# Turning attention probabilities by DMA transposes of 16-bit planes instead of TensorE transposes, in a fused attention and feed-forward kernel

## The chip, the cores and the metric

The kernel runs on one core of one Trainium2 chip. The metric is the device time of one execution in microseconds. Three runs of the kernel before gave 1068.8, 1068.5 and 1068.64 us, a median of 1068.64.

## The reference

Eight batches of eight heads, head size 64. Each head has 512 local and 32 global positions. A local query sees the 32 global keys and the local keys at most 32 positions away; a global query sees all 544 keys. The output of all heads, 512 wide, goes through a feed-forward layer of width 2048 with a squared relu.

```python
    s_g = scale * np.matmul(q_g, k_all.transpose(0, 1, 3, 2))
    out_g = np.matmul(sm(s_g), v_all)
    s_ll = scale * np.matmul(q_l, k_l.transpose(0, 1, 3, 2))
    s_ll = np.where(mask, s_ll, -1000000000.0)
    s_lg = scale * np.matmul(q_l, k_g.transpose(0, 1, 3, 2))
    s_l = np.concatenate([s_lg, s_ll], axis=-1)
    a_l = sm(s_l)
    out_l = np.matmul(a_l, np.concatenate([v_g, v_l], axis=2))
...
    h = np.maximum(x @ w_in, 0.0)
    return (h * h @ w_out).astype(np.float32)
```

All inputs are float32. The kernel multiplies mostly in a rounded 32-bit type (F32R); to keep precision it splits an operand into a rounded part and a remainder (value minus rounded value) and adds the products.

## The kernel before

The 512 local queries of a head are done in two halves, so there are 128 local work items ("heads" t in the code), each with 256 queries in two tiles of 128 and, for each tile, a window of 224 keys. The main loop (L589) runs over slots t = 0 to 145. In slot t the attention of head t goes on beside step m = t - 9 of the feed-forward layer: 17 blocks of 256 positions (16 local ones and one for all global positions) of eight steps each. A step has two first products (`gemm1`, 24 matmuls of 256 columns) and, one slot later, two second products (`gemm2`, 12 of 512 columns).

The first 16 heads are "plain": they multiply in full float32 without a split. From slot 17 on the order on TensorE (PE), VectorE (DVE) and ScalarE (ACT) is that of the program text (`FREE`); GpSimd (POOL) and the SyncE queue (SP), which issues nearly all DMAs, are ordered by the scheduler.

One head passes through these steps. `load_head` (L90) loads queries, keys and values as `raw`, 864 columns, two slots ahead; `split_head` (L125) makes the rounded copy `hi` and the remainders one slot ahead; `scores` (L139) multiplies; `softmax1` to `softmax3` (L156 to L195) add the mask and take the row maximum (DVE), scale the maximum (DVE), take exponentials with their sum (ACT) and normalize (DVE) in one of two buffers `prob`. In the next slot `transposes` (L197) turns `prob` in four TensorE transposes into the PSUM tile `pt`, `pt_split` (L202) and `pt_rest` (L217) make rounded parts `ph` (four ACT copies) and remainders (three DVE subtractions), `av` (L226) multiplies with the values in nine matmuls, and `x_evac` (L252) brings the result to SBUF as `x_h` and `x_l`, the feed-forward layer's input.

A slot's order on TensorE is: transposes of t - 1, scores of t, `gemm1` first half, `gemm1` second half, `av` of t - 1, global scores of t, `gemm2`. On DVE: `softmax1`, `pt_rest`, `softmax3`, the square, `x_evac`, the next head's split.

Global queries of four heads form a set of 128 rows, 16 sets in all. Over the slots after the set is filled come `g_soft`, `g_exp`, `g_norm`, four transposes (`g_tr`, L347) and a fifth (`g_tr_last`), their split (`g_rest`), and two times `g_av` (13 matmuls). A table of due slots and places in the slot, in the loop, gives each its position. `act1` (L459) takes the relu of the first product on ACT; the square is on ACT in six of 16 slots (`SQ`) and on DVE in the others.

Of the kernel before, what the change touches and what calls it, by code (L numbers as in the profile page):

```python
# [9 lines left out]
I32 = mybir.dt.int32  # L10
AF = mybir.ActivationFunctionType
# [10 lines left out]
PK = QC + KC + VC  # L22
# [8 lines left out]
FREE = (17, 17, 17)  # L31
LOOK = 2
SQ = (2, 3, 4, 5, 14, 15)
# [25 lines left out]
def attention_moe(  # L59
# [10 lines left out]
    pe, ve, ac = InOrder(tc, nc.tensor), InOrder(tc, nc.vector), InOrder(tc, nc.scalar)  # L70
# [19 lines left out]
    def load_head(t):  # L90
        if plain(t):
            w_take(1)
            raw = wp.tile([P, 1024], F32, tag="w", name=f"raw{t}")[:, :PK]
        else:
            raw = p2.tile([P, PK], F32, tag="raw", name=f"raw{t}")
        if t == 0:
            nc.sync.dma_start(raw[:, : QC + KC], pk[t, :, : QC + KC])
        else:
            nc.sync.dma_start(raw, pk[t])
        heads[t] = dict(raw=raw)  # L100
# [18 lines left out]
    prob = [cp.tile([P, 2 * WIN], F32, name=f"prob{i}") for i in range(2)]  # L119
# [5 lines left out]
    def split_head(t):  # L125

        hd = heads[t]
        raw = hd["raw"]
        if plain(t):
            return  # L130
        hi = p2.tile([P, PK], F32R, tag="hi", name=f"hi{t}")
        lo = p2.tile([P, QC + 192], F32R, tag="lo", name=f"lo{t}")
        ac.copy(hi, raw)
        ve.tensor_sub(lo, raw[:, KC : KC + QC + 192], f(hi[:, KC : KC + QC + 192]))
        ve.tensor_sub(hi[64:, :KC], raw[64:, :KC], f(hi[64:, :KC]))
        ve.tensor_sub(hi[32:64, PK - 64 :], raw[32:64, PK - 64 :], f(hi[32:64, PK - 64 :]))
        hd["hi"], hd["lo"] = hi, lo
# [18 lines left out]
    def softmax1(t):  # L156
        hd = heads[t]
        hf = (t // 8) % 2
        pr = prob[t % 2]
        st = p2.tile([P, 8], F32, tag="st", name=f"st{t}")  # L160
        for u in range(2):
            m = 2 * hf + u
            ve.tensor_tensor_reduce(
                out=pr[:, WIN * u : WIN * (u + 1)],
                in0=hd["s"][:, u, :],
                in1=masks[:, WIN * m : WIN * (m + 1)],
                scale=1.0,
                scalar=-3.0e38,
                op0=ALU.add,
                op1=ALU.max,  # L170
                accum_out=st[:, u : u + 1],
            )
        ve.tensor_scalar(out=st[:, 2:4], in0=st[:, 0:2], scalar1=-scale(t), scalar2=None, op0=ALU.mult)
        hd["st"] = st

    def softmax2(t):
        st = heads[t]["st"]
        pr = prob[t % 2]
        for u in range(2):
            w_ = pr[:, WIN * u : WIN * (u + 1)]  # L180
            ac.activation(
                out=w_, in_=w_, func=AF.Exp, scale=scale(t), bias=st[:, 2 + u : 3 + u], accum_out=st[:, 4 + u : 5 + u]
            )

    def softmax3(t):
        st = heads[t]["st"]
        pr = prob[t % 2]
        ve.tensor_scalar(out=st[:, 6:8], in0=st[:, 4:6], scalar1=1e-9, scalar2=None, op0=ALU.add)
        ve.reciprocal(out=st[:, 0:2], in_=st[:, 6:8])
        for u in range(2):  # L190
            w_ = pr[:, WIN * u : WIN * (u + 1)]
            if MUL <= t < NPLAIN:
                ac.activation(out=w_, in_=w_, func=AF.Copy, scale=st[:, u : u + 1])
            else:
                ve.tensor_scalar(out=w_, in0=w_, scalar1=st[:, u : u + 1], scalar2=None, op0=ALU.mult)  # L195

    def transposes(t):  # L197
        pr = prob[t % 2]
# [3 lines left out]
    def pt_split(t):  # L202
        hd = heads[t]
        if plain(t):
            pts = p2.tile([P, 512], F32, tag="gh", name=f"pts{t}")
            ac.copy(pts, pt)
            hd["pts"] = pts
            return
        ph = p1.tile([P, 640], F32R, tag="ph", name=f"ph{t}")
        pl = p1.tile([P, 256], F32R, tag="pl", name=f"pl{t}")  # L210
        ac.copy(ph[:, :256], pt[:, :256])
        ac.copy(ph[:64, 256:384], pt[:64, 320:448])
        for r in (0, 32):
            ac.copy(ph[r : r + 32, 384:640], pt[64:96, 256:512])
        hd["ph"], hd["pl"] = ph, pl

    def pt_rest(t):  # L217
        if plain(t):
            return
        ph, pl = heads[t]["ph"], heads[t]["pl"]  # L220
        ve.tensor_sub(pl, pt[:, :256], f(ph[:, :256]))
        ve.tensor_sub(ph[64:, 256:384], pt[:64, 320:448], f(ph[:64, 256:384]))

        ve.tensor_sub(ph[64:, 384:640], pt[64:, 256:512], f(ph[:64, 384:640]))

    def av(t):  # L226
# [11 lines left out]
        else:  # L238
            xa = ps_a.tile([64, HALF], F32, tag="xa", name=f"xa{t}")
            vh, vl, ph, pl = hd["hi"][:, c:], hd["lo"][:, QC:], hd["ph"], hd["pl"]  # L240
            mm = []
            for u in range(2):
                o, vs, ps = xa[:, 128 * u : 128 * u + 128], slice(64 * u, 64 * u + 64), slice(128 * u, 128 * u + 128)
                mm += [(o, vh[:, vs], ph[:, ps]), (o, vl[:, vs], ph[:, ps]), (o, vh[:, vs], pl[:, ps])]
            o = xa[:, 64:192]
            mm += [(o, vh[:, 128:192], ph[:, 256:384]), (o, vl[:, 128:192], ph[:, 256:384])]
            mm.append((xa, vh[:, 192:256], ph[:, 384:640]))
# [91 lines left out]
    def g_norm(t):  # L339
# [17 lines left out]
    def g_tr_last(t):

        if state["gs"] is None:
            state["gs"] = ps_a.tile([P, 416], F32, tag="gs", name=f"gs_{t}")  # L360
        ge = state["gs"][:, 288:]
        pe.transpose(ge, sg[:, (t // 4) % 2, 512:640], ident)
        state["ge"] = ge

    def g_rest(t):
        (pth, gt), ge = state["gpt"], state["ge"]
        ptl = p1.tile([P, 512], F32R, tag="ptl", name=f"ptl{t}")
        ac.copy(pth[:64, 512:], ge[:64, :])
        ve.tensor_sub(ptl, gt, f(pth[:, :512]))
        ve.tensor_sub(pth[64:, 512:], ge[64:, :], f(pth[:64, 512:]))  # L370
# [132 lines left out]
    def evac(blk, tiles=(0, 1)):  # L503
        for i in tiles:
            pool, tag = ((p1, "ot"), (p2, "gl"))[i]
# [83 lines left out]
    for t in range(NSTEP + LAG + 1):  # L589
        m = t - LAG  # L590
        ve.on, ac.on, pe.on = [t >= x for x in FREE]
        prev, run = 1 <= t <= NT, 0 <= m < NSTEP
        live, early = t < NT, t < NPLAIN
        if t < NPLAIN - 8:
            load_head(t + 8)
        if NPLAIN <= t + 2 < NT:
            load_head(t + 2)
        if run:
            w_need(m)
        if prev:  # L600
            transposes(t - 1)
        for job, *args in jobs.pop((t, 5), ()):
            job(*args)
        if live and not early:
            scores(t)
        if run:
            gemm1(m, 0)
        if prev:
            pt_split(t - 1)
        for job, *args in jobs.pop((t, 4), ()):  # L610
            job(*args)
        if live:
            softmax1(t)
            softmax2(t)
        if prev:
            pt_rest(t - 1)
        for job, *args in jobs.pop((t, 3), ()):
            job(*args)
# [7 lines left out]
        if prev:  # L626
            av(t - 1)
# [4 lines left out]
        if live and not early:  # L632
            softmax3(t)
        if run:
            act1(m)
        if prev:
            x_evac(t - 1)
            if plain(t - 1):
                w_take(-1)
        if early:  # L640
            softmax3(t)
        w_tick(t, 1)
        if t + 1 < NT:
            split_head(t + 1)
# [5 lines left out]
        elif t == NT:  # L650
            state["gs"] = None
        if live and t % 4 == 3 and (t // 8) % 2 == 1:
            d = t if t % 8 == 3 else t + 2
            for at, *job in (
# [116 lines left out]
```

## Time and profile before

| | |
|---|---|
| median of three runs | 1068.64 us |
| span of the profiled execution | 1067.0 us |
| PE busy | 1050.4 us (98%) |
| DVE busy | 856.3 us (80%) |
| ACT busy | 753.1 us (71%) |
| POOL busy | 3.9 us, 14 instructions |
| mean DMA rate | 91 GB/s |

The profiled execution's span runs from its first to its last instruction; the time measured from outside contains it. Busy time is the sum of an engine's instruction spans; neighbouring matmuls overlap in the pipeline, so starts, not durations, tell what a matmul costs. All instructions issued through the in-order helper carry line L52, so groups are told apart by their tiles' names. PEld is TensorE's weight load. In a row of a group, the numbers behind the bar are busy us and mean ns of one, then idle time before them and what ended it.

### The profile page before, as it was taken

The numbers are of one execution on the slowest core, as the hardware profiler recorded it, in microseconds if no ns is written. First come the engines' busy times: TensorE is split into PE (matmuls) and PEld (weight loads), VectorE is DVE, ScalarE is ACT, GpSimd is POOL, SyncE is SP. The second block draws the span as 40 slices with busy tenths as digits, with TensorE's granted clock in tenths as the row PEclk, the third lists the DMA queues.
The fourth block names the chain that finished last, engine by engine and source line by source line (L and its number), as shares of the span: only waits on it lengthen the run. The fifth ranks groups of instructions, "written<-read, shape, count | busy, mean of one in ns | idle before, by whom it ended". The sixth has DMA issues, their size and how long they took to land.

```text
span 1067.0 us, 21142 instructions
## 1 busy us (share of the span) xinstructions
PE 1050.4 (98%) x7568; PEld 941.7 (88%) x7568; DVE 856.3 (80%) x2687; ACT 753.1 (71%) x1901; POOL 3.9 (0%) x14
## 2 busy tenths in 40 slices
PE   7999999999999999999999999999999999999998
PEld 6776889999998989998999989999999989999896
DVE  5698988898888989988888888888888888874321
ACT  5898877778777776778777777777777787774322
POOL 1000000000000000000000000000000000000000
PEclk9999999999999999999999999999999999999999
DMA  9772132223222322222322222223221322201000
GB/s 372 310 263 74 57 106 76 71 80 98 68 89 64 103 65 83 74 91 77 94 71 82 86 72 76 90 66 100 78 89 55 94 86 66 88 29 33 13 20 20
DMA packets 54312, 96.78 MB, mean 91 GB/s; under 512 B 4288, under 2 KB 29376, under 8 KB 54208
## 3 DMA queue, kind: packets, MB, share of 16 engines
q1 hardware_dynamic: 54064, 95.37, 27.2%
q8 instruction: 60, 0.98, 0.4%
q14 instruction: 44, 0.36, 0.1%
q10 hardware_dynamic: 144, 0.07, 0.0%
HBM read 86.51 MB, written 8.91 MB: 89 GB/s over the span
## 4 chain that ended last, share of the span: by engine, by line
PE 87%; ACT 7%; DVE 4%; issue 1%; DMA 0%; ACTq 0%
PE o L52 33%; PE h L52 32%; PE xa L52 7%; PE s L52 6%; PE pt L52 5%; PE gxo L52 2%; PE gs L52 2%; ACT prob L52 1%; DVE prob L52 1%; ACT r L52 1%; ACT ph L52 1%; ACT hi L52 1%; ACT ot L52 1%; PE gt L52 1%; ACT sg L52 0%
## 5 line engine op out<-in xcount | busy, mean ns | idle before, releaser
L52 PE MATMUL h<-x_h,ws 128*128 128x256 f32 x2048 | 388.9, 283 | 0.0
L52 PEld LDWEIGHTS h<-x_h,ws 128*128 128x128 f32 x2048 | 327.0, 191 | 0.5
L52 PE MATMUL o<-ws,gh 128*128 128x512 f32 x1024 | 321.3, 395 | 0.0
L52 PE MATMUL h<-x_l,ws 128*128 128x256 f32 x1024 | 289.1, 282 | 0.1
L52 PEld LDWEIGHTS o<-ws,gh 128*128 128x128 f32 x1024 | 185.5, 188 | 34.6
L52 PE MATMUL o<-ws,gl 128*128 128x512 f32 x512 | 202.6, 396 | 0.0
L52 PEld LDWEIGHTS h<-x_l,ws 128*128 128x128 f32 x1024 | 195.9, 191 | 0.9 <-DVE x_l L52 0.4
L52 ACT CAST ph<-pt 128x256 fp32r<-128x256 f32 x448 | 141.1, 341 | 67.7 <-PE pt L52 60.8
L52 ACT ACTIVATE prob<-prob,st 128x224 f32<-128x224 f32 x270 | 127.8, 475 | 61.2 <-DVE st L52 59.1
L52 ACT ACTIVATE r<-h 128x512 f32<-128x512 f32 x136 | 81.4, 599 | 112.3 <-PE h L52 112.3
L52 PEld LDWEIGHTS o<-ws,gl 128*128 128x128 f32 x512 | 96.2, 188 | 22.7
L52 DVE CUSTOM_DVE_ANT_0 prob<-s,con 128x224 f32<-128x224 f32 x256 | 90.0, 386 | 24.5 <-PE s L52 23.2
L52 DVE TENSOR_TENSOR gl<-r,gh 128x512 fp32r<-128x512 f32 x128 | 87.9, 686 | 23.3 <-ACT gh L52 20.5
L52 ACT CAST hi<-raw 128x864 fp32r<-128x864 f32 x112 | 102.5, 915 | 1.4
L52 DVE TENSOR_TENSOR r<-h,r 128x512 f32<-128x512 f32 x82 | 56.7, 692 | 51.9 <-ACT r L52 50.6
L52 PE MATMUL xa<-ph,hi 128*64 128x128 f32 x448 | 87.3, 238 | 1.6 <-DVE ph L52 1.2
L52 DVE TENSOR_TENSOR hi<-raw,hi 64x352 fp32r<-64x352 f32 x224 | 82.5, 368 | 6.4
L52 ACT CAST gh<-r 128x512 fp32r<-128x512 f32 x128 | 79.1, 618 | 9.1 <-DVE r L52 8.7
L52 DVE TENSOR_TENSOR ph<-pt,ph 64x128 fp32r<-64x128 f32 x224 | 79.6, 355 | 7.0
L52 DVE TENSOR_TENSOR lo<-raw,hi 128x448 fp32r<-128x448 f32 x112 | 69.6, 622 | 15.3 <-ACT hi L52 12.5
L52 PE MATMUL pt<-con,prob 128*128 128x128 f32 (+1 forms) x512 | 78.2, 274 | 0.7 <-ACT prob L52 0.5
L52 DVE TENSOR_SCALAR prob<-prob,st 128x224 f32<-128x224 f32 x242 | 70.7, 334 | 4.1
(80 smaller groups left out, 1572.7 us busy)
## 6 DMA issues: line engine op xcount, KB each, us to landing
raw<-in_pk_dram SPq DMA_DIRECT2D x127, 432.0 KB, 3.2
wr<-in_w_dram SPq DMA_DIRECT2D x32, 512.0 KB, 7.9
gv<-in_vg_dram SPq DMA_DIRECT2D x32, 320.0 KB, 3.3
out_dram<-ot SPq DMA_DIRECT2D x32, 256.0 KB, 2.2
qr<-in_qg_dram SPq DMA_DIRECT2D x31, 64.0 KB, 2.8
out_dram<-ot SPq DMA_DIRECT2D x8, 64.0 KB, 1.7
con<-in_consts_dram SPq DMA_DIRECT2D x2, 224.0 KB, 5.1
raw<-in_pk_dram SPq DMA_DIRECT2D x1, 304.0 KB, 3.2
```

Of the source, the lines that this page charges most:

```text
L52: r = method(*args, **kwargs)
```

## The change

From the 17th head on, and for all global sets, TensorE no longer turns the probabilities. GpSimd copies the two 16-bit halves of each float32 word into two planes (`turn`), one DMA issued from SP transposes the planes, and GpSimd puts the halves together again (`join`). Local probabilities use one buffer each: `prob`, `planes`, `turned`, `joined`. ACT then makes the rounded parts with one copy of 512 columns (`parts`), DVE the remainders with three subtractions (`parts_rest`). `av` moves from the middle of the next slot to its end, behind the second `gemm2`, and `x_evac` into the slot after that. The head's split is cut into queries and keys (`split_qk`, one slot ahead, DVE remainders queued behind `parts_rest`) and values (`split_v`, in the head's own slot); `raw` is 800 columns wide. The row maximum is taken as a minimum of the negated scaled scores, so that its scaling on DVE goes. All squares are on ACT from step 8 on, in the tile `pt`. GpSimd and SP are held to the program's order from slot 17 on too, and a later head's load stands behind the transposing DMA of its slot.

```diff
-FREE = (17, 17, 17)
+FREE = (17, 17, 17, 17, 17)
-SQ = (2, 3, 4, 5, 14, 15)
...
+    def split_qk_rest(t):
+        ve.tensor_sub(hi[64:, :KC], raw[64:, :KC], f(hi[64:, :KC]))
+        ve.tensor_sub(hi[:, QK:], raw[:, KC:QK], f(hi[:, KC:QK]))
+    def split_v(t):
+        raw = heads[t]["raw"]
+        v = heads[t]["v"] = p2.tile([P, 2, 192], F32R, tag="v", name=f"v{t}")
+        ac.copy(v[:, 0, :], raw[:, QK:])
+        ve.tensor_sub(v[:, 1, :], raw[:, QK:], f(v[:, 0, :]))
...
+    def turn(t):
+        words = prob.bitcast(U16).rearrange("p (n h) -> p h n", h=2)
+        to = planes.rearrange("p (h n) -> p h n", h=2)
+        for o, a, n in ((0, 0, WIN), (256, WIN, 96), (384, 320, 128)):
+            po.tensor_copy(to[:, :, o : o + n], words[:, :, a : a + n])
+        sp.dma_start_transpose(out=turned, in_=planes)
+    def join(t):
+        words = joined.bitcast(U16).rearrange("p (n h) -> p h n", h=2)
+        po.tensor_copy(words, turned.rearrange("p (h c) n -> p h (c n)", h=2))
+    def parts(t):
+        ph = heads[t]["ph"] = p1.tile([P, 512], F32R, tag="ph", name=f"ph{t}")
+        ac.copy(ph, joined)
+    def parts_rest(t):
+        ve.tensor_sub(ph[96:, 128:384], joined[64:96, 128:384], f(ph[64:96, 128:384]))
+        ve.tensor_sub(ml[:64, :], joined[:64, 192:320], f(ph[:64, 192:320]))
+        ve.tensor_sub(pl.rearrange("p (c n) -> p c n", c=2), sides(joined), sides(f(ph)))
...
+    def g_turn(t, s):
+        a = p1.tile([P, 1280], U16, tag="pth", name=f"gp{t}")
+        z = p1.tile([P, 10, P], U16, tag="ptl", name=f"gq{t}")
+        words = s.bitcast(U16).rearrange("p (n h) -> p h n", h=2)
+        po.tensor_copy(a.rearrange("p (h n) -> p h n", h=2), words)
+        sp.dma_start_transpose(out=z, in_=a)
+        po.tensor_copy(words, z.rearrange("p (h c) n -> p h (c n)", h=2))
...
-                (d + 2, 1, g_tr),
-                (d + 3, 5, g_tr_last),
-                (d + 3, 4, g_rest),
+                (d + 3, 2, g_parts),
```

TensorE at a slot's end and the next slot's start, in the kernel before; `gl` and `gh` are the squared hidden values, `ws` weights, `s` scores, `h` the first product:

```order
L52 MATMUL o_6_5510<-ws_658,gh_5421 128x512 x2
L52 MATMUL o_6_5510<-ws_658,gl_5422 128x512
L52 MATMUL pt<-con,prob_93 128x128 x2
L52 MATMUL pt<-con,prob_93 96x128 x2
L52 MATMUL s_5533<-hi_5503 128x224
L52 MATMUL s_5533<-hi_5503,lo_5504 128x224
```

The same place in the changed kernel, where `v` holds the values:

```order
L53 MATMUL o_5_4549<-ws_1209,gh_5102 128x512 x2
L53 MATMUL o_5_4549<-ws_1209,gl_5103 128x512
L53 MATMUL xa_5187<-ph_5135,v_5018 64x128 x4
L53 MATMUL xa_5187<-ph_5135,v_5018 64x256 x2
L53 MATMUL xa_5187<-ml,v_5018 64x128
L53 MATMUL xa_5187<-pl_5169,v_5018 64x128 x2
L53 MATMUL s_5202<-qk_5165 128x224 x4
L53 MATMUL h_5212<-x_h,ws_578 128x256
```

The transposes stood between the second product and the next scores; now the value products stand there, and the scores follow them.

GpSimd in the changed kernel, at a slot that holds a global set; `gp` and `gq` are that set's planes before and after the DMA, `sg` its probabilities:

```order
L53 COPY joined<-turned 128x2x512
L53 COPY planes<-prob 128x2x224
L53 COPY planes<-prob 128x2x96
L53 COPY planes<-prob 128x2x128
L53 COPY gp_5635<-sg 128x1280
L53 COPY sg<-gq_5636 128x2x640
L53 COPY joined<-turned 128x2x512
```

Between a slot's planes and the next slot's join there is nothing else in a plain slot; with a global set both of its copies stand there, the second behind its DMA.

DVE in the changed kernel, in the slot after that, from the normalizing products on; `gvl` and `gvh` are the global values' parts, `qk` the next head's:

```order
L53 TENSOR_SCALAR prob<-prob,st_6339 128x224 x2
L53 TENSOR_TENSOR gvl_0_6375<-gv_0_6076,gvh_0_6374 128x512
L53 TENSOR_TENSOR gvh_0_6374<-gv_0_6076,gvh_0_6374 32x128
L53 TENSOR_TENSOR ph_6362<-joined,ph_6362 32x256
L53 TENSOR_TENSOR ml<-joined,ph_6362 64x128
L53 TENSOR_TENSOR pl_6397<-joined,ph_6362 128x256
L53 TENSOR_TENSOR qk_6393<-raw_6266,qk_6393 64x352
L53 TENSOR_TENSOR qk_6393<-raw_6266,qk_6393 128x256
```

The remainders of the joined tile stand ahead of the next head's split, and behind the global values' split. In the kernel before the three remainders came from PSUM and stood ahead of the normalizing products.

More of the change, by code (lines that the diff above doesn't have):

```diff
@@ L94, in load_head @@
         else:
-            raw = p2.tile([P, PK], F32, tag="raw", name=f"raw{t}")
+            raw = p2.tile([P, PS], F32, tag="raw", name=f"raw{t}")
         if t == 0:
@@ L118, in attention_moe @@
     qgz = cp.tile([P, 512], F32R, name="qgz")
-    prob = [cp.tile([P, 2 * WIN], F32, name=f"prob{i}") for i in range(2)]
+    prob = cp.tile([P, 2 * WIN], F32, name="prob")
+    planes = cp.tile([P, 1024], U16, name="planes")
+    turned = cp.tile([P, 8, P], U16, name="turned")
+    joined = cp.tile([P, 512], F32, name="joined")
+    ml = cp.tile([P, P], F32R, name="ml")
+    nc.gpsimd.memset(planes, 0)
+    nc.gpsimd.memset(f(ml), 0.0)
     pt = ps_a.tile([P, 512], F32, name="pt")
@@ L158, in softmax1 @@
         hf = (t // 8) % 2
-        pr = prob[t % 2]
+        pr = p2.tile([P, QK + QC], F32, tag="qk", name=f"pr{t}")[:, : 2 * WIN] if plain(t) else prob
+        hd["pr"] = pr
         st = p2.tile([P, 8], F32, tag="st", name=f"st{t}")
@@ L177, in softmax2 @@
         st = heads[t]["st"]
-        pr = prob[t % 2]
+        pr = heads[t]["pr"]
         for u in range(2):
@@ L186, in softmax3 @@
         st = heads[t]["st"]
-        pr = prob[t % 2]
+        pr = heads[t]["pr"]
         ve.tensor_scalar(out=st[:, 6:8], in0=st[:, 4:6], scalar1=1e-9, scalar2=None, op0=ALU.add)
-        ve.reciprocal(out=st[:, 0:2], in_=st[:, 6:8])
+        ve.reciprocal(out=st[:, 2:4], in_=st[:, 6:8])
         for u in range(2):
@@ L217, in pt_rest, with pt_copy @@
[L217 to L224, printed above, removed]
+    def pt_copy(t):
+        pts = p2.tile([P, 512], F32, tag="gh", name=f"pts{t}")
+        ac.copy(pts, pt)
+        heads[t]["pts"] = pts
+    def turn(t):
[4 more added lines that the diff above has]
+        sp.dma_start_transpose(out=turned, in_=planes)
@@ L595, in attention_moe @@
             load_head(t + 8)
+        if run:
+            w_need(m)
+        old = prev and plain(t - 1)
+        new = prev and not old
+        if old:
+            transposes(t - 1)
+        if new:
+            join(t - 1)
+        if live and not early:
+            scores(t)
+        if old:
+            pt_copy(t - 1)
+        if live:
+            softmax1(t)
+        if NPLAIN <= t - 2 < NT:
+            x_evac(t - 2)
+        if run:
+            gemm1(m, 0)
+        if live and not early:
+            split_v(t)
+        if live:
+            softmax2(t)
+        if new:
+            parts(t - 1)
+        if live and not early:
+            softmax3(t)
+            turn(t)
         if NPLAIN <= t + 2 < NT:
             load_head(t + 2)
[L598 to L618, printed above, removed]
+        for place in (4, 3):
+            for job, *args in jobs.pop((t, place), ()):
+                job(*args)
         if 0 < m <= NSTEP and m % 8 == 1 and m > 8:
@@ L631, in attention_moe @@
             scores(t + 1)
-        if live and not early:
-            softmax3(t)
+        if t + 1 < NT and not early:
+            split_qk(t + 1)
         if run:
             act1(m)
-        if prev:
+        if old:
             x_evac(t - 1)
-            if plain(t - 1):
-                w_take(-1)
+            w_take(-1)
         if early:
```

120 lines of the change are left out of this document (51 added, 69 removed).

## The prediction

> **What bounds the kernel now.** I read the page first, then the busy time by stretches, then one tile (the transposed probabilities, for the length of a slot), then the timeline of single slots, and last the groups with their shapes kept apart, for prices.
>
> ```profile
> span 1067.0 us, 21142 instructions
> PE 87%; ACT 7%; DVE 4%; issue 1%; DMA 0%; ACTq 0%
> 500.00:600.00 100.00, 99.79 (x758) 91.26 (x757) 87.62 (x277) 73.15 (x191) 0.00 (x0) 1.00 0.25 77
> L52 PE MATMUL xa<-ph,hi x448: 220/223/306, 110.7 to 961.9; 128*64 128x128 f32 x112, 128*64 128x256 f32 x38
> ```
>
> The second line is the chain that ended last: TensorE holds 87% of it. In the stretch from 500 to 600 us the columns are PE, weight loads, DVE, ACT and POOL busy, then the granted clock (1.00) and the DMA share: TensorE never rests, DVE is busy 87.6%, ACT 73.2%, GpSimd not at all. The value products run from 110.7 to 961.9 us, which is 111 slots of 7.67 us. So an instruction taken off TensorE is worth its time, as long as nothing makes TensorE wait.
>
> ```profile
> 445.09 0.60 PE L52 MATMUL pt<-con,prob 128*128 128x128 f32 x4
> 452.38 0.60 PE L52 MATMUL gt<-con,sg 128*128 128x128 f32 x4
> 452.82 0.60 PE L52 MATMUL pt<-con,prob 128*128 128x128 f32 x4
> 602.38 0.22 PE L52 MATMUL xa<-ph,hi 128*64 128x128 f32 x1
> 602.54 0.17 DVE L52 TENSOR_SCALAR st<-st 128x2 f32<-128x2 f32 x1
> 602.86 0.28 PE L52 MATMUL xa<-ph,hi 128*64 128x256 f32 x1
> 602.94 0.58 DVE L52 TENSOR_SCALAR prob<-prob,st 128x224 f32<-128x224 f32 x2
> 602.98 0.30 PE L52 MATMUL gs<-hi,qgz 128*128 128x288 f32 x1
> 607.04 0.19 PEld L52 LDWEIGHTS s<-hi 128*128 128x128 f32 x1
> 607.59 0.29 PE L52 MATMUL h<-x_h,ws 128*128 128x256 f32 x1
> 607.79 0.39 DVE L52 CUSTOM_DVE_ANT_0 prob<-s,con 128x224 f32<-128x224 f32 x1 [0.81 <-PE s L52]
> 608.74 0.48 ACT L52 ACTIVATE prob<-prob,st 128x224 f32<-128x224 f32 x1
> 609.59 0.18 ACT L52 ACTIVATION_READ_ACCUMULATOR prob<-prob,st 128x1 f32 x1
> ```
>
> Starts are in the first column. A slot without work for the global rows is 452.38 - 445.09 = 7.29 us. The four transposes of a set hold TensorE from 452.38 to 452.82, 0.44 us. The eight value products of 128 columns start within 602.38 to 602.86, 0.06 us apart; the one of 256 takes 0.12 until the next instruction. From a slot's start (607.04, its scores) the row maximum begins at +0.75, the exponentials at +1.70 and end at +2.73.
>
> **The change, part by part.**
>
> ```profile
> L52 DVE TENSOR_TENSOR lo<-raw,hi 128x448 fp32r<-128x448 f32 x112 | 69.6, 622 | 15.3 <-ACT hi L52 12.5
> L52 DVE TENSOR_TENSOR hi<-raw,hi 64x352 fp32r<-64x352 f32 x112 | 58.5, 522 | 3.2
> L52 DVE TENSOR_TENSOR pl<-pt,ph 128x256 fp32r<-128x256 f32 x112 | 47.1, 421 | 2.8 <-ACT ph L52 1.9
> L52 DVE TENSOR_TENSOR ph<-pt,ph 64x256 fp32r<-64x256 f32 x112 | 47.8, 427 | 3.5
> L52 DVE TENSOR_TENSOR ph<-pt,ph 64x128 fp32r<-64x128 f32 x112 | 31.7, 283 | 3.5
> L52 DVE TENSOR_TENSOR hi<-raw,hi 32x64 fp32r<-32x64 f32 x112 | 24.1, 215 | 3.2
> L52 DVE TENSOR_TENSOR r<-h,r 128x512 f32<-128x512 f32 x82 | 56.7, 692 | 51.9 <-ACT r L52 50.6
> L52 DVE TENSOR_TENSOR gvl<-gv,gvh 128x512 fp32r<-128x512 f32 x32 | 22.1, 692 | 9.3 <-ACT gvh L52 8.8
> L52 DVE TENSOR_TENSOR x_l<-xa,x_h 64x256 fp32r<-64x256 f32 x120 | 49.6, 414 | 14.8 <-ACT x_h L52 12.9
> L52 ACT CAST hi<-raw 128x864 fp32r<-128x864 f32 x112 | 102.5, 915 | 1.4
> L52 ACT CAST ph<-pt 128x256 fp32r<-128x256 f32 x448 | 141.1, 341 | 67.7 <-PE pt L52 60.8
> L52 ACT ACTIVATE r<-r 128x512 f32<-128x512 f32 x54 | 34.1, 632 | 1.6
> L52 ACT CAST gh<-r 128x512 fp32r<-128x512 f32 x128 | 79.1, 618 | 9.1 <-DVE r L52 8.7
> L52 ACT CAST gvh<-gv 128x640 fp32r<-128x640 f32 x32 | 23.0, 718 | 0.0
> L121 POOL MEMSET qgz<- 128x512 f32 x1 | 0.5, 524 | 0.3 <-POOLq L761 0.3
> L122 POOL MEMSET sg<- 128x64 f32 x1 | 0.2, 152 | 0.0
> L278 POOL COPY qz<-qr 128x128 f32<-128x128 f32 x4 | 1.2, 292 | 25.0 <-DMA qr<-in_qg_dram 25.0
> raw<-in_pk_dram SPq DMA_DIRECT2D x127, 432.0 KB, 3.2
> wr<-in_w_dram SPq DMA_DIRECT2D x32, 512.0 KB, 7.9
> gv<-in_vg_dram SPq DMA_DIRECT2D x32, 320.0 KB, 3.3
> out_dram<-ot SPq DMA_DIRECT2D x32, 256.0 KB, 2.2
> ```
>
> Taken off TensorE: 112 local sets x 0.44 = 49.3 us, and 16 global ones of five transposes (0.44 + 0.11), 8.8 us. Added: the value products are now seven of 128 columns and two of 256, 0.06 us more x 112 = 6.7 us. A plain slot would be 7.29 - 0.44 + 0.06 = 6.91 us.
>
> In their place stands a loop over three engines, with one buffer at each station. GpSimd copies the probabilities into two planes of 16 bits (three copies, 448 + 192 + 256 = 896 elements), SP issues the transposing DMA of 256 KB, and GpSimd joins the halves at the next slot's start (1024 elements). No row shows a 16-bit copy. The memsets give (524 - 152) / 448 = 0.83 ns an element; the copy of 128 elements, 292 ns, gives 2.28 if all of it scales. I take 0.83 ns and the copy's remainder, 0.18 us each, since a copy streams as a memset does: 1.29 us to plane, 1.03 us to join. The outer end is 1920 x 2.28 = 4.4 us for both. No row shows a transposing DMA either: plain ones land after 2.2 us (256 KB) to 3.3 us (320 KB), and 7.9 in the crowded start. I take 2.8 us, and 3.0 for the 320 KB of a global set; it could be below the 2.2, since no HBM is in it.
>
> The Trainium skill (VectorE: DVE Perf Modes, The three transpose paths) speaks against the change: 1309 ns for a 128x128 block by DMA against 390 ns on TensorE. TensorE's starts here are 0.11 us apart, far under its figure. Eight blocks in series at that price would be an estimated 10.5 us and a slot near 13, some 600 us more over the kernel; no run here shows it.
>
> Does the loop fit? The separate scaling of the maximum goes, so the exponentials end near +2.5. From 602.54 to the end of the two normalizing products is 0.98 us, so the first half is ready at +3.2, the second at +3.5. Planes +4.5, landing +7.3, join 8.35, which is +1.44 of the next slot. ACT rounds the joined tile (512 columns, 0.62), DVE does its three remainders (0.43 + 0.28 + 0.42 = 1.13) and, queued behind them, the next head's two (0.52 + 0.42 = 0.94), on which the next scores wait. So the join may end as late as 6.91 - 2.69 = +4.2. Plain slots are covered, with 2.8 us to spare there, and 1.76 us before GpSimd must be free for the next planes (+3.2). If the cover is gone, each us too many in the loop costs 112 us.
>
> Global sets lack that cover. GpSimd does copy, wait, copy between two local sets: planes +4.5, global copy (1280 elements) 5.75, landing 8.75, copy back 10.0, join 11.0, that is +4.1. In that slot ACT rounds the value chunk (0.72) and DVE takes 0.69 + 0.28 for it, ahead of the late remainders: ACT 4.7 and 5.45, DVE 6.4, 7.55, 8.5, where 6.91 is due: 1.6 us late. Fourteen to sixteen sets, about 24 us; at the prices above it runs from nothing to 3 us a set.
>
> The heads' x evacuation moves to two slots later, behind the row maximum. On DVE it ends at about 0.75 + 2 x 0.35 + 0.41 = +1.9; the first step of a block needs it at its eleventh product, 0.55 + 10 x 0.12 = +1.75. Some 0.2 us, 14 blocks, 3 us.
>
> The load of the head two ahead is moved past SP's transposing DMA: issued near +4.9, landed (3.2) at +1.2, read after +2.0 by ACT. It is covered; if SP stands waiting for GpSimd, it slips with the loop. DVE loses 0.17 (scaled maximum), 0.20 (622 to 421, 448 to 256 columns), 0.22 and on average 0.43 (ten of 16 products of 692 ns become squares on ACT), and gains 0.34 for the values (192 columns, between 283 and 421): 87.6% of 7.67 is 6.72, so 6.04 us a slot. ACT exchanges 0.92 + 4 x 0.34 = 2.28 for 0.69 (608 columns, between 618 and 718), 0.32 (192 columns, by the 341 of 256), 0.62 and 10/16 x 0.63 = 0.39, together 2.02. Both have room, so these count nothing. The first sixteen heads keep TensorE's transposes and lose only the scaled maximum, 16 x 0.17 = 2.7 us of DVE at most: nothing.
>
> Sum: 1067.0 - 49.3 - 8.8 + 6.7 + 24 + 3 = 1042.6 us of span. The three runs' median, 1068.64, lies 1.64 above the span: 1044.2, said as 1045.
>
> **The rivals.** *The loop sets the slot (slower).* It decides when planes, DMA and join pass 6.9 us, and costs when they pass about 7.3, that is with a DMA over 4.6 to 5 us at my copies, or over 2.5 at the 2.28 ns ones. For it speaks that every station has one buffer and that GpSimd waits in line; against it every plain DMA row after the start but for its 7.9. Priced with 1.0 ns an element and a DMA of 5 us: 2.65 + 5 + 0.2 = 7.85 us for 98 slots (0.2 for the hand-overs), and for 14 with a global set 4480 elements, six copies' 0.18 and a DMA of 5.3 + 0.2, 11.1 us; 925 us against 112 x 7.67 = 859: +66, 1134 us.
>
> *GpSimd and DVE stop each other.* About half of DVE's work per slot (the next head's remainders 0.94, values 0.34, three remainders 1.13, two products 0.6, of 6.04) reads two SBUF operands or is a product from SBUF to SBUF; GpSimd's 2.6 us fall among it. If each us of overlap stops one of them, DVE loses half of 2.6: 7.35 us a slot, and with 0.5 of its present 0.95 us idle 7.85: 112 x 0.18 = +20, about 1088. It decides from 0.7 us a slot. GpSimd is idle in the trace, so nothing speaks for or against. By the Trainium skill (SBUF — State Buffer) the two share a port pair that one holds for a whole instruction, against such DVE operations; no run here shows it yet.
>
> *All is covered*, the global sets too: 1042.6 - 24 + 1.6 = 1020.
>
> **How the numbers follow.** Forecast 50%, all covered 10%, loop 27%, port 13%. The likeliest time is 1045, its own range 1022 to 1066. The range that should hold 8 in 10 leaves out the last of the covered case and the loop at its slowest: 1022 to 1125. 0.2% (2.1 us) is about what a measurement of this kernel can tell from no change. Faster: 0.60. Of the two slower cases' 40%, 5 land within 0.2%: same 0.05, slower 0.35.
>
> **What would show it.** Right: plain slots of 6.9 us, the transposing DMA landing in under 3.5 us, ACT's wait for the joined tile under 0.5 us in plain slots, and TensorE idle chiefly before value products or scores one slot after a global set, 1 to 2 us each. Wrong: GpSimd busy or waiting through the whole slot with plain slots over 7.3 us (the loop), GpSimd copies or DVE remainders lasting well beyond their present rows (the port), or the first products of a block waiting by far more than 0.2 us.

## The result and the profile after

The changed kernel takes 1124.93 us (median of four runs, 1123.84 to 1125.87) where the kernel before takes 1068.71 on the same chip: a ratio of 1.0526, 95% interval 1.0511 to 1.0541. It is slower by 56 us; the forecast was 1045, faster. The page of the kernel after, its head, its chain and its transposing DMA:

```profile
span 1122.1 us, 20557 instructions
PE 1052.1 (94%) x7040; PEld 927.1 (83%) x7040; DVE 829.5 (74%) x2477; ACT 720.4 (64%) x1743; POOL 373.6 (33%) x496
PEclk9999989999999989989899999989899999989999
PE 62%; DVE 14%; DMA 8%; ACT 6%; issue 6%; POOL 2%; SPq 0%; DVEq 0%; POOLq 0%; ACTq 0%
PE h L53 24%; PE o L53 23%; DMA gq<-gp 6%; PE s L53 6%; PE xa L53 5%; DVE prob L53 3%; PE gxo L53 2%; POOL joined L53 2%; DVE qk L53 2%; DVE ml L53 2%; PE gs L53 1%; DVE x_l L53 1%; DMA raw<-in_pk_dram 1%; DVE pl L53 1%; DVE st L53 1%
turned<-planes SPq DMA_TRANSPOSE x112, 3.0
```

TensorE held 87% of the chain that ended last; now it holds 62%, and 6% of the span, about 67 us, stands on one transfer of which there are only 16: `gq<-gp`, the global sets' transposing DMA. The local one, `turned<-planes`, of which there are 112, is not on that line. PE's busy time even grew by 1.7 us, though TensorE no longer turns any of these: the row of its granted clock has eights now, and matmuls at a lower clock are longer.

The starts of four consecutive slots (their scores) in the kernel after, the last of them the slot behind a global set, and the two that follow:

```profile
583.30 0.65 PE L53 MATMUL s<-qk 128*128 128x224 f32 x4
590.24 0.65 PE L53 MATMUL s<-qk 128*128 128x224 f32 x4
597.20 0.65 PE L53 MATMUL s<-qk 128*128 128x224 f32 x4
604.14 1.05 PE L53 MATMUL s<-qk 128*128 128x224 f32 x4
615.88 1.44 PE L53 MATMUL s<-qk 128*128 128x224 f32 x4 [0.22 <-DVE qk L53]
625.51 0.65 PE L53 MATMUL s<-qk 128*128 128x224 f32 x4
```

Three slots of 6.94 to 6.96 us, then one of 11.74 and one of 9.63. The slots repeat in a cycle of 16 (the eight heads of a batch in two halves, with two global sets). The table gives the median length of each over the steady part, from the starts of the scores, and as a whole cycle the sum of the 16 medians; d + 3 is the slot behind the one in which a set's probabilities are ready, and "A" and "B" are the two sets of a cycle.

| kernel | A: d + 3, d + 4, d + 5 | B: d + 3, d + 4, d + 5 | plain | whole cycle | time |
|---|---|---|---|---|---|
| before | 8.60, 7.34, 7.26 | 8.39, 7.34, 7.27 | 7.28 | 122.27 | 1068.7 |
| after | 11.21, 9.67, 6.95 | 11.41, 9.99, 6.95 | 6.95 | 128.81 | 1124.9 |
| `e1_global_unturned` | 6.95, 7.88, 6.96 | 6.95, 7.85, 6.95 | 6.95 | 116.43 | 1033.9 |
| `e2_join_first` | 8.20, 8.19, 6.96 | 9.56, 8.15, 6.95 | 6.95 | 121.87 | 1073.3 |
| `e8_join_first_pieces` | 7.07, 9.10, 6.96 | 6.95, 8.81, 6.98 | 6.95 | 119.40 | 1056.2 |
| `e9b_rest_before_next_scores` | 7.06, 7.32, 8.15 | 6.96, 7.35, 8.35 | 6.95 | 117.33 | 1041.2 |

So the plain slots came out as forecast, and all that was lost, and more, was lost in two slots of each global set. What happens in them, in the timeline of the kernel after (start, duration, engine; in brackets how long the engine had been idle and what ended that):

```profile
600.59 1.53 POOL L53 COPY planes<-prob 128x448 uint16<-128x448 uint16 x3 [0.93 <-DVE prob L53]
602.07 1.64 POOL L53 COPY gp<-sg 128x1280 uint16<-128x1280 uint16 x1
602.15 1.23 SPq L53 DMA_TRANSPOSE turned<-planes  x1
602.62 1.92 DVE L53 TENSOR_TENSOR qk<-raw,qk 64x352 fp32r<-64x352 f32 x2
603.47 0.53 SPq L53 DMA_DIRECT2D raw<-in_pk_dram  x1
604.09 1.32 SPq L53 DMA_TRANSPOSE gq<-gp  x1
608.99 1.64 POOL L53 COPY sg<-gq 128x1280 uint16<-128x1280 uint16 x1 [5.28 <-DMA gq<-gp]
610.54 1.32 POOL L53 COPY joined<-turned 128x1024 uint16<-128x1024 uint16 x1
611.90 0.62 ACT L53 CAST ph<-joined 128x512 fp32r<-128x512 f32 x1 [4.98 <-POOL joined L53]
612.57 0.45 PE L53 MATMUL xa<-ph,v 128*64 128x128 f32 x4 [1.56 <-ACT ph L53]
613.17 0.69 DVE L53 TENSOR_TENSOR gvl<-gv,gvh 128x512 fp32r<-128x512 f32 x1 [5.24 <-ACT gvh L53]
614.19 0.42 DVE L53 TENSOR_TENSOR ph<-joined,ph 32x256 fp32r<-32x256 f32 x1
614.67 0.45 PE L53 MATMUL xa<-ph,v 128*64 128x256 f32 x2 [1.65 <-DVE ph L53]
615.29 0.98 DVE L53 TENSOR_TENSOR qk<-raw,qk 64x352 fp32r<-64x352 f32 x2
```

Read it from the middle. At 604.09 SP issues the set's DMA; GpSimd has nothing it may do but its copy back, and stands for 5.28 us. Behind that copy in GpSimd's order is the local `joined`, whose own planes were issued at 602.15 and, at 3.0 us, had landed by about 605. It starts at 610.54. ACT stood for 4.98 us until it was joined, DVE for 5.24 behind ACT, and TensorE, out of `gemm2` at 611.0, waits twice on the way to the next scores at 615.88. (The `qk` subtractions at 602.62 come up again under "Pieces alone".) The waits of the whole kernel after say the same (us in total, times, longest):

```profile
POOL sg L53 <- DMA gq<-gp: 90.3, 16, 10.2
ACT ph L53 <- POOL joined L53: 81.4, 37, 7.8
DVE gvl L53 <- ACT gvh L53: 75.5, 16, 8.0
```

The slot after that, at 9.63, has no such wait. The busy time by stretches of the kernel after shows another loss (columns PE, weight loads, DVE, ACT, POOL, then the granted clock):

```profile
583.30:590.24 6.94, 6.94 (x53) 6.36 (x52) 5.82 (x19) 5.45 (x14) 3.15 (x4) 1.00 0.52 125
611.00:615.00 4.00, 0.79 (x8) 0.52 (x7) 1.75 (x5) 3.07 (x6) 1.98 (x4) 1.00 0.22 42
616.00:617.00 1.00, 0.92 (x4) 0.73 (x5) 0.99 (x3) 0.69 (x2) 0.81 (x1) 0.63 0.93 338
617.00:618.00 1.00, 1.00 (x7) 1.00 (x7) 1.00 (x1) 0.00 (x0) 1.00 (x1) 0.50 1.09 332
618.00:619.00 1.00, 1.00 (x6) 1.00 (x6) 0.97 (x3) 0.00 (x0) 0.08 (x1) 0.50 0.08 22
619.00:620.00 1.00, 1.00 (x8) 1.00 (x7) 0.94 (x6) 0.77 (x3) 0.00 (x0) 0.66 0.00 0
620.00:624.00 4.00, 4.00 (x34) 3.61 (x33) 3.77 (x11) 3.59 (x11) 1.78 (x3) 1.00 0.00 0
```

TensorE works 0.79 of the 4 us from 611 to 615. From 616 its granted clock is 0.63, 0.50, 0.50, 0.66, and 1.00 again from 620: 0.37 + 0.50 + 0.50 + 0.34 = 1.7 us of full speed gone, after the wait is over. A plain slot has 1.00 throughout (first row).

### The profile page after: what moved, and what is told of

The parts are those of the page before. It is cut to its first block, busy times and chain, and to the rows that moved or that the text cites. A ratio compares the mean times of both kernels' runs of the same rounds, so it can differ in the third digit from the quotient of the medians.

```text
span 1122.1 us, 20557 instructions
## 1 busy us (share of the span) xinstructions
PE 1052.1 (94%) x7040; PEld 927.1 (83%) x7040; DVE 829.5 (74%) x2477; ACT 720.4 (64%) x1743; POOL 373.6 (33%) x496
## 4 chain that ended last, share of the span: by engine, by line
PE 62%; DVE 14%; DMA 8%; ACT 6%; issue 6%; POOL 2%; SPq 0%; DVEq 0%; POOLq 0%; ACTq 0%
PE h L53 24%; PE o L53 23%; DMA gq<-gp 6%; PE s L53 6%; PE xa L53 5%; DVE prob L53 3%; PE gxo L53 2%; POOL joined L53 2%; DVE qk L53 2%; DVE ml L53 2%; PE gs L53 1%; DVE x_l L53 1%; DMA raw<-in_pk_dram 1%; DVE pl L53 1%; DVE st L53 1%
## 5 line engine op out<-in xcount | busy, mean ns | idle before, releaser
L53 POOL COPY joined<-turned 128x1024 uint16<-128x1024 uint16 x112 | 158.8, 1418 | 321.0 <-DMA turned<-planes 123.8
L53 POOL COPY planes<-prob 128x448 uint16<-128x448 uint16 x336 | 163.3, 523 | 189.6 <-DVE prob L53 189.6
L53 DVE TENSOR_TENSOR gl<-pt,gh 128x512 fp32r<-128x512 f32 x128 | 88.1, 688 | 83.1 <-ACT gh L53 80.9
L53 PE MATMUL xa<-ph,v 128*64 128x128 f32 (+1 forms) x672 | 77.4, 247 | 46.6 <-DVE ph L53 24.2
L53 ACT CAST ph<-joined 128x512 fp32r<-128x512 f32 x112 | 68.3, 610 | 81.7 <-POOL joined L53 81.4
L53 ACT ACTIVATE pt<-h 128x512 f32<-128x512 f32 x128 | 74.5, 582 | 70.0 <-PE h L53 69.1
L53 DVE TENSOR_TENSOR qk<-raw,qk 64x352 fp32r<-64x352 f32 x224 | 113.0, 504 | 7.8 <-ACT qk L53 0.8
L53 PE MATMUL s<-qk 128*128 128x224 f32 x448 | 89.5, 314 | 6.2 <-DVE qk L53 3.7
L53 ACT CAST qk<-raw 128x608 fp32r<-128x608 f32 x112 | 78.2, 698 | 9.6 <-DMA raw<-in_pk_dram 9.5
L53 PEld LDWEIGHTS s<-qk 128*128 128x128 f32 x448 | 66.1, 202 | 16.3 <-DVE qk L53 15.3
```

The lines of the kernel that those rows point to most:

```text
L53: r = method(*args, **kwargs)
```

## The experiments

The letters in the expectations: theory Q says that the loss is GpSimd's order, the copy back standing ahead of the next join, and the wait for that DMA with what hangs on it. Theory P says that DVE and GpSimd stop each other; P2, that this goes by whole instructions, so that shorter copies stop DVE for less. Rival L says that the loop of planes, DMA and join sets every slot. Ratios are to the kernel before on the same chip.

**Without the global way.** Undoes one part and leaves the work out.

```diff
@@ g_norm
-        g_turn(t, s)
```

> The global probabilities are not turned at all (both GpSimd copies and the DMA of each of the 16 sets are left out, so the global rows of the output are not the reference's); everything local stays. Theory Q (GpSimd's queue holds the next join behind the global set's DMA; that is where the loss lies): the two slots after each set fall from about 11.2 and 9.8 us to about 7.0 and 7.75, some 6.3 us for each of 15 sets, 1125 - 95 = about 1030 us. Rival L (the local loop itself is too long): stays over 1090. Rival P (GpSimd and DVE stop each other in every slot): stays over 1090, as 32 of about 480 copies go.

1033.91 us, ratio 0.9674 (0.9660 to 0.9689), granted clock 0.999. Both slots behind a set shrink to 6.95 and 7.88 us (the table). So 1124.9 - 1033.9 = 91 us belong to the global sets' copies and DMA, 6.1 us for each of the 15 behind slot 17, and the local way is no loss at all: without the global one the kernel is 35 us under the kernel before.

**The local join twice.** Doubles the suspected cost of rival L: the same copy again, 1.4 us a slot.

```diff
@@ join
-        po.tensor_copy(words, turned.rearrange("p (h c) n -> p h (c n)", h=2))
+        for _ in range(2):
+            po.tensor_copy(words, turned.rearrange("p (h c) n -> p h (c n)", h=2))
```

> The change with the join's copy done twice, 1.4 us more of GpSimd in each of 112 slots. If plain slots are covered as the prediction has it: GpSimd's loop in a plain slot now takes 1.4 (join) + 1.2 (planes) + 3.2 (DMA) and has 0.9 us idle before the planes; 0.9 of the 1.4 is hidden and about 0.3 us a slot shows, slots of 7.2 us, 1125 + 30 = about 1155 us. If the loop already sets the slot (rival L): 112 x 1.4 = 157 us more, about 1280 us. If GpSimd has no part in plain slots: 1125 us.

1211.93 us, ratio 1.1337 (1.1320 to 1.1354): 87 us more than the change, 0.78 a slot, between the two expectations. Its groups and waits:

```profile
L53 POOL COPY joined<-turned 128x1024 uint16<-128x1024 uint16 x224 | 313.7, 1400 | 332.3 <-DMA turned<-planes 198.5 <-DVE st L53 67.1 <-DVE gl L53 20.1
ACT ph L53 <- POOL joined L53: 217.9, 91, 9.4
```

Of a cycle's seven plain slots three take the added 1.4 us and stay at 6.94 to 6.95, two grow to 7.41 and 7.57, and two, in which ACT also copies a finished block's output (`ot`), to 8.61 and 10.24; other slots pass it on too (one from 7.45 to 8.49). So the loop does not set the plain slots of the change, but in many slots less than 1.4 us of room is left, where the prediction gave the plain slots 2.8. The longer join also stops DVE (beside it the two normalizing products, 0.58 us in a plain slot of the change, take up to 1.49), so the 87 us are not the loop's length alone.

**Matmuls into the wait.** Thirty matmuls without use stand ahead of the value products behind a set, so that TensorE does not rest.

```diff
@@ av
+        if not plain(t) and t % 16 in (3, 13) and t > 18:
+            for _ in range(30):
+                pe.matmul(xa, whi[0][:, :64], whi[1][:, :HALF], start=True, stop=True, skip_group_check=True)
```

> As the change, but in the slot after each global set 30 idle matmuls of 256 columns (30 x 0.12 = 3.6 us, results overwritten) stand on TensorE ahead of the late value products, where it now stands idle. If the halved clock after that idle time is a loss of its own (theory C): the granted clock stays near 1.0, the following slot falls from about 9.8 to about 8.1 us, 15 x 1.7 = 25 us less: about 1100 us. If it is not (the wait alone counts): 1125 us or a little more.

1114.39 us, ratio 1.0426 (1.0410 to 1.0441), mean clock 0.994 where the change has 0.963. The slot behind one set, by stretches:

```profile
610.00:614.00 4.00, 3.75 (x34) 3.42 (x33) 3.54 (x8) 3.79 (x8) 0.78 (x2) 1.00 0.67 145
614.00:618.00 4.00, 4.00 (x31) 3.83 (x30) 3.82 (x12) 1.60 (x6) 1.24 (x1) 1.00 0.36 111
```

The clock stays at 1.00 and slot d + 4 falls from 9.67 and 9.99 us to 8.54 and 8.18: the halved clock is shown as that slot's cost, 1.1 to 1.8 us. But 10.5 us came back and not 25, since two slots later a slot grew from 8.26 to 9.12 and another from 7.76 to 8.14. The first of the two begins a block of the feed-forward layer, and such first products wait 7.4 us in all for `x_l` in this run and 3.2 in the change: while TensorE was slow, that wait was partly covered.

**The join first.** Only the order: the copy back is queued behind the next join and planes, its reader one place later.

```diff
@@ g_turn, the table
-        po.tensor_copy(words, z.rearrange("p (h c) n -> p h (c n)", h=2))
+        state["gz"] = words, z
+    def g_back(t):
+        words, z = state["gz"]
+        po.tensor_copy(words, z.rearrange("p (h c) n -> p h (c n)", h=2))
...
-                (d + 3, 2, g_parts),
+                (d + 3, 3, g_back),
+                (d + 3, 1, g_parts),
```

> Same work; only GpSimd's second copy of a global set is queued one slot later, behind the next join and the next planes, and the global split at that slot's end. Theory Q: the wait for the global DMA no longer stands before a join, so TensorE does not wait: 1025 to 1045 us. Rivals L and P, and a rival D (the global DMA itself slows the local one on the shared DMA engines): little change, 1100 to 1125 us.

1073.31 us, ratio 1.0038 (1.0024 to 1.0052): 52 of the 91 us return by order alone, and the clock is 0.995. The expectation of 1025 to 1045 is missed by 28 us. Its timeline shows what stood in place of the wait:

```profile
328.00 1.45 POOL L53 COPY gp<-sg 128x1280 uint16<-128x1280 uint16 x1
328.36 1.22 DVE L53 TENSOR_TENSOR ml<-joined,ph 64x128 fp32r<-64x128 f32 x1
335.87 1.83 POOL L53 COPY sg<-gq 128x1280 uint16<-128x1280 uint16 x1
336.23 1.56 DVE L53 TENSOR_TENSOR ml<-joined,ph 64x128 fp32r<-64x128 f32 x1
590.22 0.32 DVE L53 TENSOR_TENSOR ml<-joined,ph 64x128 fp32r<-64x128 f32 x1
```

The subtraction `ml` takes 0.32 us in a plain slot. Beside either global copy it takes 1.22 and 1.56, and ends with the copy (329.58 and 329.45; 337.79 and 337.70).

**The same, in pieces.** `e2_join_first` with each global copy cut into five of 256 elements.

```diff
@@ g_turn, g_back
-        po.tensor_copy(a.rearrange("p (h n) -> p h n", h=2), words)
+        for o in range(0, 640, 128):
+            po.tensor_copy(a.rearrange("p (h n) -> p h n", h=2)[:, :, o : o + 128], words[:, :, o : o + 128])
...
-        po.tensor_copy(words, z.rearrange("p (h c) n -> p h (c n)", h=2))
+        for c in range(5):
+            po.tensor_copy(
+                words[:, :, 128 * c : 128 * c + 128], z.rearrange("p (h c) n -> p h c n", h=2)[:, :, c, :]
+            )
```

> As e2_join_first, with both GpSimd copies of a global set cut into five of 256 elements. In e2 a DVE remainder that stood beside such a copy took 1.2 to 1.6 us in place of 0.3 and ended with it. Theory P2 (an operation of DVE with two SBUF inputs stands still for the whole of a GpSimd copy): it now waits for a piece only, 0.3 to 0.4 us, and some 1 us a set comes back, 1073 - 15 = about 1058 us. Rival: the wait is for bandwidth and not for the instruction: 1073 us or more, as five copies have five starts.

1056.17 us, ratio 0.9881 (0.9867 to 0.9896). In its timeline:

```profile
332.54 3.02 POOL L53 COPY sg<-gq 128x256 uint16<-128x256 uint16 x5
332.89 0.39 DVE L53 TENSOR_TENSOR ml<-joined,ph 64x128 fp32r<-64x128 f32 x1
```

GpSimd needs 3.02 us where one copy took 1.83, yet the kernel wins 17 us: `ml` slips in between two pieces, and slot d + 3 is at 7.07 and 6.95. P2 is confirmed here; the 17 us are what is left of it after slot d + 4 has grown by 0.9 and 0.7. The slot d + 4, 9.10 and 8.81 us, still waits, now for the product that reads the block copied back (the local value products wait until `gxs`, that product's copy out of PSUM, has emptied the tile that both use):

```profile
PEld xa L53 <- ACT gxs L53: 15.1, 15, 1.3
```

**Pieces alone.** The change itself, with the copies cut and no order touched.

```diff
@@ g_turn
-        po.tensor_copy(a.rearrange("p (h n) -> p h n", h=2), words)
+        for o in range(0, 640, 128):
+            po.tensor_copy(a.rearrange("p (h n) -> p h n", h=2)[:, :, o : o + 128], words[:, :, o : o + 128])
         sp.dma_start_transpose(out=z, in_=a)
-        po.tensor_copy(words, z.rearrange("p (h c) n -> p h (c n)", h=2))
+        for c in range(5):
+            po.tensor_copy(
+                words[:, :, 128 * c : 128 * c + 128], z.rearrange("p (h c) n -> p h c n", h=2)[:, :, c, :]
+            )
```

> The change as it is, with nothing but GpSimd's two global copies cut into five pieces each; no queue is reordered. If the lock of VectorE by whole copies takes its share by itself: about 1 us in each of 15 sets, 1105 to 1115 us. If the wait for the next join behind the copy back sets the length of these slots (theory Q), the lock lies inside that wait and nothing is returned: 1120 to 1128 us.

1130.25 us, ratio 1.0570 (1.0556 to 1.0585), 5 us over the change. Where GpSimd's order keeps the join waiting, DVE has time to stand, and the longer copies make that wait longer: slot d + 3 is at 11.94 and 11.68. The lock is not free in the change as it is, though. In its timeline above the two `qk` subtractions at 602.62, beside the first global copy, take 1.92 us where those at 615.29 take 0.98, and the scores at 604.14 wait for them; with the copies in pieces TensorE's weight loads for the scores wait 9.6 us in all for `qk` in place of 15.3, and the slot before d + 3 of set A falls from 7.44 to 7.03. That is less than the longer copies take; once the order is mended the pieces gain 17 us.

**Global sets back on TensorE, two ways.** First the transposes into the scores' PSUM tile, read there by ACT and DVE:

```diff
@@ g_parts, the table
+        gt = ps_a.tile([P, 512], F32, tag="s", name=f"gt{t}")
+        for c in range(4):
+            pe.transpose(gt[:, 128 * c : 128 * c + 128], s[:, 128 * c : 128 * c + 128], ident)
...
-                (d + 3, 3, g_split_v, 0),
-                (d + 3, 2, g_parts),
+                (d + 2, 2, g_split_v, 0),
+                (d + 3, 4, g_parts),
```

> The global sets are turned by TensorE again (five transposes into PSUM, between the two halves of the first product), local ones by DMA as in the change. Theory Q: all of the loss goes and 16 x 0.55 = 9 us of TensorE come back, with some wait for the copies out of PSUM: 1030 to 1050 us. Rivals L and P: over 1090 us.

1063.18 us, ratio 0.9948 (0.9933 to 0.9963); slot d + 3 is 9.04 and 10.08. The waits name the new place:

```profile
PEld gt L53 <- DVE st L53: 18.0, 15, 3.0
PEld gs L53 <- DVE pth L53: 11.3, 13, 1.7
```

The transposes wait until the row maximum has emptied the tile, the global scores until DVE has read theirs. Then with the transposes behind the scores, in the tile `pt`, and two ACT copies that empty it at once:

```diff
@@ the table; g_back copies pt to sg on ACT
+                (d + 3, 5, g_tr),
+                (d + 3, 4, g_back),
                 (d + 3, 3, g_split_v, 0),
```

> Local by DMA; global sets by TensorE into the PSUM tile of the squares, after the scores, when that tile is free, and copied back by two ACT copies (0.6 and 0.25 us), all else as in the change. Theory Q: the loss of the sets goes, TensorE takes 9 us again: 1040 to 1050 us, faster than both kernels.

1049.16 us, ratio 0.9816 (0.9802 to 0.9831): the local part of the change alone is 20 us faster than the kernel before.

**The kernel before with the global part alone.** Twice: with the value products where they stood, then a slot later. The first edit takes the change's `g_turn` and `g_parts` into the kernel before, and puts the global values' split with them at the slot's end; the second moves one product and what follows it:

```diff
@@ the kernel before: g_norm, the table
+        g_turn(t, s)
...
-                (d + 2, 1, g_tr),
-                (d + 3, 5, g_tr_last),
-                (d + 3, 4, g_rest),
-                (d + 3, 3, g_split_v, 0),
+                (d + 3, 2, g_split_v, 0),
+                (d + 3, 2, g_parts),
...
@@ the second
-                (d + 3, 1, g_av, 0),
-                (max(d + 4, 17), 3, g_x, 0),
+                (d + 4, 0, g_av, 0),
+                (max(d + 5, 17), 3, g_x, 0),
```

> The kernel before, with local probabilities turned by TensorE as ever, and only the global sets turned by GpSimd copies and DMA. Theory Q (the loss comes from the join that stands behind the global DMA in GpSimd's queue): with no join in that queue the long way costs nothing, and the five transposes a set go from TensorE, 16 x 0.55 = 9 us: 1058 to 1069 us. If turning a global set that way is dear by itself (its 4.6 us landing, or DVE stopped during the copies): 1080 us or more.

> The kernel before with only the global sets turned by GpSimd and DMA, as in e5, but the global value products stand a whole slot later, behind the end of the long way (about 10.5 us). Theory Q (the loss comes from products that stand where the turned planes cannot have arrived): the wait goes, and what is left is the 16 sets' own saving on TensorE and ScalarE against a little lock on VectorE: 1058 to 1069 us, at most the time before. Rival (the copies and the DMA of a global set cost the time themselves, wherever they are read): 15 sets by 1 us or more, over 1080 us.

1121.54 us, ratio 1.0489 (1.0472 to 1.0507), and 1091.06, ratio 1.0209 (1.0195 to 1.0223). Here GpSimd and SP have no local copies, and the DMA lands in 3.0 us; still the first of them loses 52 us, far from what Q expected. Its waits name the product that stands too early:

```profile
PEld gxo L53 <- ACT pth L53: 14.1, 15, 1.5
PEld gxo L53 <- DVE ptl L53: 13.6, 15, 0.9
PEld gxo L53 <- DVE gvl L53: 10.7, 14, 0.8
```

Its mean clock is 0.977, so the wait brings the low clock with it here too. Standing a slot later it gives 30 us back, at a clock of 0.999, but not all: Q's 1058 to 1069 is missed again, and the rival's bound, over 1080, holds. Part of the rest is the lock, now on the feed-forward layer's own subtraction. The later kernel first, then the kernel before:

```profile
337.95 1.58 DVE L53 TENSOR_TENSOR gl<-r,gh 128x512 fp32r<-128x512 f32 x1
```

```profile
330.58 0.67 DVE L52 TENSOR_TENSOR gl<-r,gh 128x512 fp32r<-128x512 f32 x1
```

That is 0.9 us of DVE beside the copy back; slots d + 3 and d + 4 together are 17.44 and 17.91 us against 15.94 and 15.73. Another part stands in slot d + 4: DVE does the four subtractions of the global values and of the turned block, from 345.54 on, ahead of the next row maximum, which so starts 2.8 us after its scores (348.19 and 345.41), where it starts 0.7 after them in the kernel before (340.36 and 339.62). That is the place to which this edit moved the split, and no run moves it back, so what each part is worth stays open.

**Everything mended.** `e8_join_first_pieces` with the turned block's readers a slot later still; the second of the two kernels has its remainders one place earlier. In the first, in every second set, the remainders are taken after the next global scores have been written over the block, so that its global rows are not the reference's.

```diff
-                (d + 3, 1, g_parts),
-                (d + 4, 0, g_av, 0),
-                (max(d + 5, 17), 3, g_x, 0),
+                (d + 4, 3, g_parts),
+                (d + 4, 2, g_parts_rest),
+                (d + 5, 4, g_av, 0),
+                (max(d + 6, 17), 3, g_x, 0),
...
@@ the second
-                (d + 4, 2, g_parts_rest),
+                (d + 4, 5, g_parts_rest),
```

> e8 (1056.2 us) with the global value products one slot later, and ScalarE's and VectorE's splitting of the global block moved with them. What e8 had left in the slot after next was 8.8 to 9.1 us against 7.76, 1.2 us in each of 15 sets, waiting for the copy back and ScalarE's split. If that wait was for a product that stood too early: 1056 - 15 x 1.2 = 1038 us, 1036 to 1045, with everything turned by DMA as in the change. Rival (ScalarE and GpSimd have no more room in these slots, so the wait only moves): 1052 to 1058 us.

> e9 with VectorE's remainders of the turned global block taken before the next batch's global scores are written over that buffer (in e9 every second set took them after, so the global rows there are not the reference's). The same instructions, one of them earlier in VectorE's order, in the slot two after the set's. If that order costs nothing: 1038 to 1043 us, as e9 (1040.0). Rival (the remainders now wait for ScalarE's split ahead of the next tile's splits): up to 0.5 us in each of 15 sets, 1048 us.

1040.04 us, ratio 0.9733 (0.9719 to 0.9746), and 1041.21 us, ratio 0.9741 (0.9728 to 0.9755); the second computes what the kernel before computes, with all turning by DMA. Its page:

```profile
span 1038.2 us, 20711 instructions
PE 1013.4 (98%) x7040; PEld 899.5 (87%) x7040; DVE 821.9 (79%) x2477; ACT 723.0 (70%) x1743; POOL 417.9 (40%) x624
```

TensorE is busy 98% again, and 1041.21 - 1033.91 = 7 us are left of the 91.

## Why the prediction was wrong

The step that failed is the term for the global sets, as the prediction put it: "Global sets lack that cover ... 1.6 us late ... about 24 us", with an end of 3 us a set. The mechanism is right, in the order and place named there. Its size is not: the sets' way cost 91 us, 6.1 in each of 15 sets, and that turned a gain into a loss. That 1124.9 lies just inside the range of 1022 to 1125 is luck, since the upper end came from the loop rival.

- *Where the sum went off.* Counted from its slot's start, 597.20, the set's stations were forecast and then measured so: planes done +4.5 and +4.9; global copy 5.75 and 6.5; landing 8.75 and 11.8; copy back 10.0 and 13.4; join 11.0 and 14.7. So the join is 3.7 us later than forecast, and 2.3 of these come in between copy and landing: 3.0 us had been taken, from plain DMA rows, and 5.28 passed. SP was not in the sum: the set's DMA stood 0.4 us behind the local one and a load, and its copy back could start 4.9 after SP took it, where such a DMA lands in 3.0 with neither just ahead of it (`e5_only_global_by_DMA`); which of the two holds it was not taken apart. Of the other 1.4 us, GpSimd's copies make 1.3: 1.53, 1.64, 1.64 and 1.32 for 1.29, 1.25, 1.25 and 1.03.
- *What is late next.* The scores came at 615.88, 11.74 us into the slot, 4.8 late where 1.6 was forecast.
- *What no term had.* TensorE's clock falls behind such a wait and takes 1.7 us more from the next slot. That the prediction priced a wait at its own length was a mistake in kind; the fillers show the second part apart from the first, at 10.5 us of the kernel's time in all.
- *Plain slots: right.* 6.95 us against 6.91. The loop's parts were all under-priced: planes 0.57 + 0.43 + 0.57 = 1.57 for 1.29, join 1.42 for 1.03, DMA 3.0 for 2.8, together 6.0 for 5.1; the room behind the join swallowed 0.9 us. The memset's 0.83 ns an element was too little: the join takes 1.42 us for 1024. The Trainium skill's 1309 ns a block (VectorE: DVE Perf Modes, The three transpose paths) is not what a column of eight costs here: eight blocks land 3.0 us after their issue.
- *The loop rival: wrong.* Its 1134 us is near the result, but by a different way; the plain slots show none of it, and with the loop 1.4 us longer three of the seven still do not.
- *The port rival: right as a mechanism, wrong in its place.* It put the loss into every slot. In plain slots DVE is stopped too (in the one from 590.24 to 597.20 the values' subtraction takes 1.08 us beside the join, where at 606.41, with no copy running, it takes 0.34), but it has the time, and the slot is 6.96. Beside the global copies of 1.5 to 1.8 us it counts: 17 us, once the wait is gone.
- *The x evacuation: right in place, up to twice the size.* TensorE's first products wait 3.2 us in all for `x_l` in the change, where 3 had been put, and 5.8 where the long waits are gone. The row of the change, then that of `e1_global_unturned`:

```profile
PE h L53 <- DVE x_l L53: 3.2, 13, 0.7
```

```profile
PE h L53 <- DVE x_l L53: 5.8, 13, 1.2
```

- *All covered* would have been 1020. Without any global turning the runs show 1034: 5.84 us less a cycle where 16 x 0.38 + 2 x 0.55 = 7.2 was due, 9.5 over seven cycles. The waits for `x_l`, 5.8 us where the sum had 3, are some of it; the rest was not taken apart.

What each mending gave back, in order: 52 us for the join ahead of the copy back, 17 for copies in pieces, 15 for the readers a slot later, 7 not returned. The first step also moved the reader by a place, and the second lengthened the copies, so the shares belong to this order.

## What to carry to other kernels

When a step leaves an engine for a longer way round (copy, queue, DMA, copy), the question is not only how long that way is but what stands behind it on each in-order engine that it uses: put the part that waits behind the work that is ready, and its reader a whole way later. A rare step can cost more than a frequent one: 16 long ways took 91 us, 112 shorter ones took none. And price a wait of TensorE of several us with what follows it, the clock.

## What the runs showed of the hardware

- *The clock.* 0.79 us of work in 4 us is followed by a granted clock of 0.50 for 3.41 us (616.26 to 619.67 in the change), 1.7 us lost; with the gap filled it stays at 1.00. The Trainium skill (TensorE: Matmul & The Clock Gate, Part 1: The HAM clock gate) has an idle window of about 3.4 us halve the rate, until about as long a busy one has passed; the trace agrees with the second length. The first it does not bear out, and the measurement decides: TensorE's longest rest in this wait is 1.65 us, and in the 3.41 us ahead of the halving it was busy for 1.47, so here the clock fell without a rest of that length.
- *The lock.* A subtraction of two SBUF operands goes from 0.32 to 1.22 and 1.56 us and from 0.67 to 1.58 beside one GpSimd copy of 1280 elements, and ends 0.1 us (`ml`) and 0.5 us (`gl`) behind it; between copies of 256 `ml` takes 0.39. The Trainium skill (SBUF — State Buffer, SBUF: two separate sides) says that such an operation and a GpSimd one take the shared ports for a whole instruction; the trace agrees, and cutting the copy is the remedy that the runs add.
- *The transposing DMA.* 256 KB inside SBUF land 3.0 us after issue; 320 KB take 3.0 in `e5_only_global_by_DMA` and 4.6 as the median in the change, where they follow the local one and a load on SP.
- *GpSimd's 16-bit copies.* 1024 elements take 1.42 us in the change; five copies of 256 take 3.02 where one of 1280 takes 1.64 to 1.83, so each further start costs an estimated 0.3 us, (3.02 - 1.83) / 4.
